# Attention with its queries, keys and values laid out by the host, in a fused attention and mixture-of-experts kernel

## The chip, the cores and the metric

One core of one Trainium2 chip runs the whole program. The metric is device time in microseconds (us). The engines: PE is TensorE (matmuls; PEld its weight loads), DVE is VectorE, ACT is ScalarE, POOL is GpSimd, SP is SyncE, which here only issues transfers. PSUM is the memory that PE writes, SBUF the working memory.

## What is computed

Attention of 2 batches, 8 heads, 576 positions and head size 64 under a mask of blocks of 64, then a gated feed-forward layer, then a mixture of eight experts. Only the inputs of the attention change their form.

```python
def _attn_ref(q, k, v):                      # each (2, 8, 576, 64), float32
    scores = scale * np.matmul(q, k.transpose(0, 1, 3, 2))     # scale = 1/8
    scores = np.where(block_i >= block_j, scores, -1000000000.0)
    scores = scores - np.max(scores, axis=-1, keepdims=True)
    attn = np.exp(scores)
    attn = attn / (np.sum(attn, axis=-1, keepdims=True) + 1e-09)
    return np.matmul(attn, v)
...
x = attn_out as (1152, 512)
x = (x @ w_a) * (x @ w_b) @ w_out            # weights float64, d_ff 1536
return _moe2_ref(x, w_gate, w1, w2, capacity)  # 8 experts, the best one of each token
```

## The kernel before, in words

The program has four stages: attention, the two products with `w_a` and `w_b` (line 418, `prod`), the product with `w_out` (L571), and the experts. PE is the engine that all of them lean on.

**Attention.** Two heads share the 128 partitions, so there are eight *pairs* n = 0 to 7. The host's arrays have positions outside and the 64 head elements inside, whereas a score product needs the head elements on the partitions. So `load_pair` (L166) brings q, k and v in with three transfers each (pieces of 64 elements, 256 bytes); `turn` (L184) turns q or k on PE by five transposes into a PSUM tile `pt`; `q_put` (L191) copies q from there to SBUF on ACT and scales it, `k_put` (L195) copies k on DVE. Then, per pair, four *units* u of score rows, one tile of PSUM each: unit 0 is row tiles 0 and 2, unit 1 is tile 1, unit 2 is tile 3, unit 3 is the last half tile. `score` (L199) makes them on PE, `smax` (L233) takes the row maxima on DVE, `sexp` (L246) the exponentials and sums on ACT into `PB`, `recip` (L263) the reciprocals on DVE, `norm` (L269) multiplies on POOL. Seven groups g of transposes of `PB` (`xpose`, L302) go to PSUM tiles `pT` and are copied to `PTa`/`PTb` by `x_put` (L319): groups 2, 4, 6 on ACT, the rest on DVE. `pv` (L331) multiplies with the values in seven runs; `o_hi` (L348, ACT) and `o_lo` (L352, DVE) write the result split in two parts, `xTh` and `xTl`.

**Rooms.** The pool `psD` has two buffers of two PSUM banks; every score unit, every turned q or k, and the two early products below take one of them in turn. `PB` has two buffers, turned q and k two each, raw q and k three.

**The order is written out by hand** in the table `ORDER`: each word is one step, a letter and its numbers (`steps` in the listing: L load_pair, q/k turn, Q q_put, K k_put, s score, m smax, e sexp, r recip, n norm, t xpose, h x_put, p pv, O o_hi, P o_lo). `s12` is pair 1, unit 2; `p06` is the last run of pair 0's values; `p76` the last of the attention. Each engine does its own part of the words in this order, and waits by itself for what it needs.

**Weights.** `w_a` and `w_b` are float64 read as pairs of int32. Column block f takes `a` (load_wab, two transfers into a `raw` tile of two buffers), `b` (ACT), four DVE steps `c` (`bits64`: L365, L367, L371, L375), `H` (ACT, L402) and `I` (POOL, L408). Blocks 0, 1 and 2 are done among the attention's words. `E0` and `E1` (`ahead`) are the first thirds of the products of blocks 0 and 1, 24 matmuls each, in a `psD` buffer.

**The stage after it** goes over blocks f and thirds c. Per third, PE makes 24 matmuls into two PSUM tiles of three buffers each; `gate_mul` copies one on ACT (`asb`, L486) and multiplies with the other on DVE (`g_sb`, L487), which frees them. The same engines prepare the next blocks of weights there, and `w_out` too (`wor`, `wob`, `woh`: a load, one ACT step, four DVE steps, an ACT cast at L380). The loads of block 3 and of the first `w_out` part stand on SP's queue behind the transfer of `wg_sb`, whose room is that of the attention's tiles.

Of the kernel before, what the change touches and what calls it, by code (L numbers as in the profile page):

```python
# [30 lines left out]


ORDER = """
L00 L01 L10 L11 q0 k0 Q0 L20 K0 q1 s01 Q1 L21 m01 s03 e01 L02 m03 s00 e03 s02 L30 r03 m00 n04 m02 e00 L31 t06
L12 e02 k1 r00 n00 K1 h06 n01 k2 r02 L40 s11 K2 n02 t00 m11 s13 L41 h00 e11 n03 t01 m13 s10 L22 h01 e13 t02 m10
t03 h02 L32 s12 h03 e10 r13 t04 m12 n14 a0 t05 p00 h04 h05 p01 p02 e12 r10 p03 n10 p04 O00 n11 r12 p05 P00 p06
q2 n12 O01 L42 t10 P01 Q2 t11 h10 k3 n13 L50 s21 h11 K3 t16 m21 s23 h16 L51 e21 t12 m23 t13 b0 s20 a1 h13 h12
c00 t14 e23 t15 m20 h14 p10 s22 h15 e20 r23 p11 m22 p12 n24 p13 O10 r20 p14 e22 c01 n20 p15 p16 P10 q3 n21 L52
c02 O11 t26 Q3 n22 k4 P11 h26 s31 r22 L60 b1 K4 t20 n23 t21 m31 s33 h20 L61 e31 h21 p20 c03 s30 m33 H0 a2 t22
m30 t23 e33 I0 p21 h23 h22 s32 r33 O20 c10 e30 t24 n34 t25 P20 p22 m32 h24 p23 q4 h25 e32 t36 r30 L70 c11 p24  # L40
n30 h36 r32 p25 n31 c12 p26 Q4 k5 L71 O21 q5 n32 b2 K5 t30 P21 t31 s41 Q5 L62 h30 n33 s43 h31 m41 c13 p30 e41
t32 m43 t33 H1 s40 c20 h32 I1 p31 h33 e43 t34 m40 O30 t35 h34 s42 P30 e40 h35 p32 r43 p33 m42 n44 p34 s51 r40
e42 c21 n40 p35 p36 m51 t46 n41 L72 O31 c22 s53 e51 n42 P31 h46 t40 m53 s50 h40 e53 r42 t41 m50 s52 n43 p40 h41
e50 r53 p41 m52 n54 t42 t43 c23 h42 k6 e52 t44 h43 p42 r50 t45 h44 K6 n50 q6 O40 h45 t56 n51 H2 p43 P40 r52 n52
h56 p44 Q6 p45 p46 t50 O41 n53 s61 P41 s63 h50 m61 I2 t51 m63 e61 t52 p50 h51 h52 s60 e63 t53 r63 m60 t54 n64
s62 h54 h53 e60 t55 m62 t66 p51 p52 h55 h66 p53 r60 e62 p54 n60 p55 n61 p56 O50 k7 r62 O51 P50 q7 n62 P51 t60 K7
Q7 t61 h60 n63 s71 h61 s73 m71 e71 p60 m73 t62 e73 t63 s70 h62 h63 r73 s72 n74 m70 t64 m72 e70 t65 p61 p62 h65
p63 e72 t76 r70 n70 E0 h64 n71 r72 O60 h76 n72 P60 n73 t70 t71 h70 p64 h71 p65 p66 t72 O61 t73 P61 h72 p70 h73
t74 t75 h74 p71 h75 p72 O70 p73 P70 p74 p75 p76 E1 O71 P71
"""  # L50


# [13 lines left out]
@with_exitstack  # L66
def fused_kernel(ctx: ExitStack, tc, q, k, v, w_a, w_b, w_out, w_gate, w1, w2, consts, out, cap):
    nc = tc.nc
    B, H, S, D = q.shape
# [4 lines left out]
    BLK = 64
    NB = S // BLK
    NP = H // 2
    NPAIR = B * NP
# [69 lines left out]
    PB, V2, QK = [], [], []
    for s in range(3):
        t = att1.tile([P, 2, NTT, 2, D], F32, name=f"QK{s}")
        nc.vector.memset(t[BLK:, :, NQ], 0.0)  # L150
        QK.append(t)
# [12 lines left out]
    qkv, qT, kT, two, one, soft, pxs, ptx = {}, {}, {}, {}, {}, {}, {}, {}

    def load_pair(n, j):  # L166
        b, p = divmod(n, NP)
        if j == 0:
            qkv[n] = QK[n % 3]
        src = (q, k, v)[j]  # L170
        t = V2[n % 4] if j == 2 else qkv[n][:, j]
        full = S // P
# [6 lines left out]
        eng.dma_start(
            out=t[0:S % P, full, :, :],  # L180
            in_=src[b, 2 * p:2 * p + 2, full * P:S, :].rearrange("h p d -> p h d"),
        )

    def turn(n, j):  # L184
        t = qkv[n]
        pt = psD.tile([P, 1024], F32, tag="two", name=f"pt{n}_{j}")
        for tt in range(NTT):
            nc.tensor.transpose(pt[:, tt * P:tt * P + P], t[:, j, tt].rearrange("p h d -> p (h d)"), ident)
        two[n, j] = pt[:, 0:S]
# [862 lines left out]
```

## Time and profile before

| | |
|---|---|
| median of 3 runs | 511.78 us (510.99 to 513.92) |
| the profiled execution: its time / its span | 514.79 us / 513.0 us |
| granted PE clock over the span | 0.958 of full speed |
| busy: PE / DVE / ACT / POOL | 466.8 / 257.8 / 189.6 / 127.4 us |
| turning transposes L188: matmuls, busy | 80, 14.1 us |
| `k_put` L197 on DVE / `q_put` L193 on ACT | 6.0 us / 5.3 us |

The span is what the trace covers, the time is what the run took, 1.8 us more. PE's matmuls overlap in the trace, so the busy time of a group is more than the room it takes on PE; that room is read from one start to the next in a list in order of time.

### The profile page before, as it was taken

Reading aid. Unit: us, or ns where it says so; the run is one execution under the profiler, and the core shown is the slowest. Engines: PE = TensorE matmul, PEld = TensorE weight load, DVE = VectorE, ACT = ScalarE, POOL = GpSimd, SP = SyncE. Lnnn points to the kernel's source line nnn. Section 1 sums busy time; section 2 is a strip of 40 time slices with the busy share of each in tenths; the row PEclk is TensorE's granted clock in tenths of the full one; section 3 lists DMA queues with packets and bytes.
Section 4 is the critical chain, followed back from the end, with each engine's and each line's share of the span. In section 5 each row is a group of like instructions: output and inputs, shape, how many; then the busy total and the mean of one; then the engine's idle time right before and its main releaser. Section 6 shows DMA issues by size and latency. Waiting matters only on the chain. (4 is left out here: it accounts for less than half of the span.)

```text
span 513.0 us, 7684 instructions
## 1 busy us (share of the span) xinstructions
PE 466.8 (91%) x2808; PEld 376.8 (73%) x2808; DVE 257.8 (50%) x513; ACT 189.6 (37%) x391; POOL 127.4 (25%) x134
## 2 busy tenths in 40 slices
PE   5799899999998999999999999996297988999994
PEld 3466556678998999999997777773296787796541
DVE  2679997743647475655332544544365091260111
ACT  2477777643333333332231232221253271341211
POOL 1445777430313131313010110011110120102111
PEclk9799999999998999999999999999577998999998
DMA  8656510005446464654009910000796280451990
GB/s 166 156 154 164 151 26 2 1 1 167 164 145 225 145 225 145 227 205 144 1 2 371 383 44 22 21 26 2 226 289 252 60 315 20 146 221 57 348 324 5
DMA packets 67481, 73.70 MB, mean 144 GB/s; under 512 B 31410, under 2 KB 43826, under 8 KB 67424
## 3 DMA queue, kind: packets, MB, share of 16 engines
q1 hardware_dynamic: 64624, 69.26, 42.2%
q0 software_dynamic: 1456, 3.29, 1.7%
q8 instruction: 29, 0.48, 0.4%
q10 hardware_dynamic: 1344, 0.44, 0.4%
q14 instruction: 28, 0.23, 0.2%
HBM read 62.58 MB, written 11.72 MB: 145 GB/s over the span
## 5 line engine op out<-in xcount | busy, mean ns | idle before, releaser
L418 PE MATMUL p<-xTh,hi 128*128 128x384 f32 x272 | 91.8, 338 | 3.3 <-ACT asb L486 2.1
L418 PE MATMUL p<-xTl,hi 128*128 128x384 f32 x272 | 91.7, 337 | 0.0
L418 PE MATMUL p<-xTh,lo 128*128 128x384 f32 x272 | 91.6, 337 | 0.0
L278 POOL TENSOR_TENSOR PB<-PB,rs 128x576 f32<-128x576 f32 (+4 forms) x40 | 52.4, 1334 | 43.7 <-DVE rs L267 35.7
L418 PEld LDWEIGHTS p<-xTh,hi 128*128 128x128 f32 x272 | 51.6, 190 | 4.2 <-ACT asb L486 2.8
L418 PEld LDWEIGHTS p<-xTh,lo 128*128 128x128 f32 x272 | 51.6, 190 | 0.0
L418 PEld LDWEIGHTS p<-xTl,hi 128*128 128x128 f32 x272 | 51.5, 189 | 0.0
L571 PE MATMUL py<-woh,gh 128*128 128x512 f32 x108 | 45.4, 421 | 0.0
L865 PE MATMUL pH<-xt,whi 128*128 128x288 f32 x192 | 42.1, 313 | 2.8 <-ACTq L910 1.2
L571 PE MATMUL py<-woh,gl 128*128 128x512 f32 x108 | 42.5, 394 | 0.0
L571 PE MATMUL py<-wol,gh 128*128 128x512 f32 x108 | 42.3, 391 | 0.0
L897 PE MATMUL pO<-whi,ht 128*128 128x512 f32 (+1 forms) x112 | 40.1, 428 | 0.0
L253 ACT ACTIVATE PB<-sc,nm 128x256 f32<-128x256 f32 (+3 forms) x64 | 33.1, 531 | 17.7 <-DVE nm L242 12.2
L211 PE MATMUL sc<-k,q 64*64 64x288 f32 (+4 forms) x192 | 36.4, 487 | 2.6 <-ACT PB L258 1.3
L865 PEld LDWEIGHTS pH<-xt,whi 128*128 128x128 f32 x192 | 33.1, 201 | 4.4 <-ACTq L910 1.6
L381 POOL TENSOR_TENSOR wol<-wob,woh 128x1024 fp32r<-128x1024 f32 x6 | 14.4, 2406 | 86.5 <-ACT woh L380 86.5
L242 DVE TENSOR_REDUCE nm<-sc 128x2 f32<-128x512 f32 (+4 forms) x40 | 31.2, 802 | 8.7 <-PE sc L218 4.8
L408 POOL TENSOR_TENSOR lo<-bits,hi 128x1024 fp32r<-128x1024 f32 x12 | 28.7, 2389 | 24.7 <-ACT hi L402 24.7
L487 DVE TENSOR_TENSOR g_sb<-asb,p 128x384 f32<-128x384 f32 x34 | 18.3, 551 | 30.4 <-PE p L418 16.4
L839 POOL DMA_INDIRECT out<-y,ti x12 | 11.4, 946 | 87.9 <-ACT y L904 62.7
L776 DVE TENSOR_TENSOR wlo<-wraw,whi 128x1024 fp32r<-128x1024 f32 x24 | 29.1, 1222 | 6.6 <-ACT whi L775 6.5
L309 PE MATMUL pT<-cst,PB 128*128 128x128 f32 x200 | 29.9, 285 | 0.6 <-POOL PB L278 0.6
(130 smaller groups left out, 789.2 us busy)
## 6 DMA issues: line engine op xcount, KB each, us to landing
wraw<-in_moe_w SPq DMA_DIRECT2D x32, 1024.0 KB, 11.4
raw<-in_moe_w_a SPq DMA_DIRECT2D x12, 512.0 KB, 3.9
raw<-in_moe_w_b SPq DMA_DIRECT2D x12, 512.0 KB, 5.9
wor<-in_moe_w_out SPq DMA_DIRECT2D x6, 1024.0 KB, 6.8
xdisp<-zrow SPq DMA_DIRECT2D x6, 774.0 KB, 7.7
out<-zrow SPq DMA_DIRECT2D x3, 768.0 KB, 7.6
QK<-in_q SPq DMA_DIRECT2D x16, 128.0 KB, 2.6
V<-in_v SPq DMA_DIRECT2D x16, 128.0 KB, 2.8
```

What stands on the lines that cost most here:

```text
L211: nc.tensor.matmul(dst, lhsT=qT[n][hs, P * i:min(P * i + P, S)], rhs=kT[n][hs, c0:c0 + cw], start=True, stop=(i == LAST), skip_group_check ...
L242: nc.vector.tensor_reduce(out=soft[n][0][:, c:c + cnt], in_=view, op=ALU.max, axis=AX.X if i < NQ else AX.XY, negate=True)
L253: nc.scalar.activation(out=dst[:, h], in_=view[:, h], func=AF.Exp, bias=nm[:, c + h:c + h + 1], accum_out=sm[:, c + h:c + h + 1],)
L278: nc.gpsimd.tensor_tensor(out=x, in0=x, in1=r, op=ALU.mult)
L309: nc.tensor.transpose(pt[:, j * P:(j + 1) * P], tile_at(n, i, kt, h), ident)
L408: nc.gpsimd.tensor_tensor(out=lo, in0=f32(m), in1=f32(hi), op=ALU.subtract)
L418: nc.tensor.matmul(ps, lhsT=lt, rhs=rt, start=(n_ == 0), stop=(n_ == len(seq) - 1))
L487: nc.vector.tensor_tensor(out=g_sb[:, f, c * CH:(c + 1) * CH], in0=asb, in1=pb, op=ALU.mult)
L571: nc.tensor.matmul(s["py"], lhsT=lt[:, f], rhs=rt[:, f], start=(f == 0 and i == 0), stop=(f == NF - 1 and i == 2))
L776: nc.vector.tensor_tensor(out=lo[:, a:a + 2], in0=raw[:, a:a + 2], in1=f32(hi[:, a:a + 2]), op=ALU.subtract)
L865: nc.tensor.matmul(ph[:, 0:n].rearrange("p (g c) -> p g c", c=G), lhsT=lt, rhs=rt, start=(n_ == 0), stop=(n_ == len(seq) - 1),)
L897: nc.tensor.matmul(po[:2 * m if tail else m], lhsT=lt, rhs=rt, start=(f == 0 and i == 0), stop=(f == KF2 - 1 and i == len(seq) - 1),)
```

## The change

The host lays out q and k as (pair, 128 partitions of head elements, 576 positions), and v as (pair, position in tile, tile, head, element) with zeros behind the last half tile. Each is then loaded by one transfer, in one piece of 2304 or 2560 bytes per partition. `turn`, `q_put` and `k_put` are gone with their PSUM tiles. The scale of q is a step `Q` in place: on ACT for pair 0, on POOL (`tensor_scalar`, 128x576) for the others. q and k have four buffers each. The clearing of tile ends (DVE for q and k, POOL for v) falls away. `ORDER` is a new table: a pair's units now mostly come as 2, 0, 1, 3, and `E1` stands ahead of the last pair's later transposes.

```diff
 ORDER = """
-L00 L01 L10 L11 q0 k0 Q0 L20 K0 q1 s01 Q1 L21 m01 s03 e01 L02 m03 s00 e03 s02 L30 r03 m00 n04 m02 e00 L31 t06
...
+L00 L01 L10 L11 L20 Q0 L21 s02 Q1 L02 s00 m02 L30 Q2 m00 e02 L31 a0 e00 s01 r02 n03 m01 e01 s03 Q3 r00 s12 L12
...
     def load_pair(n, j):
-        b, p = divmod(n, NP)
...
-        eng = nc.scalar if (n, j) == (0, 1) else nc.sync
-        for h in range(2):
-            eng.dma_start(
-                out=t[:, 0:full, h, :],
-                in_=src[b, 2 * p + h, 0:full * P, :].rearrange("(t p) d -> p t d", p=P),
-            )
...
-    def turn(n, j):
...
-    def q_put(n):
-        qT[n] = att.tile([P, S], F32, tag="q", name=f"q{n}")
-        nc.scalar.activation(out=qT[n], in_=two.pop((n, 0)), func=AF.Copy, scale=scale)
-
-    def k_put(n):
-        kT[n] = att.tile([P, S], F32, tag="k", name=f"k{n}")
-        nc.vector.tensor_copy(out=kT[n], in_=two.pop((n, 1)))
+
+        if j == 2:
+            nc.sync.dma_start(out=V2[n % 4], in_=v[n])
+            return
+        t = att.tile([P, S], F32, tag="qk"[j], name=f"{'qk'[j]}{n}", bufs=4)
+        (nc.scalar if (n, j) == (0, 1) else nc.sync).dma_start(out=t, in_=(q, k)[j][n])
+        (qT, kT)[j][n] = t
+
+    def q_scale(n):
+        if n == 0:
+            nc.scalar.mul(out=qT[n], in_=qT[n], mul=scale)
+        else:
+            nc.gpsimd.tensor_scalar(out=qT[n], in0=qT[n], scalar1=scale, scalar2=None, op0=ALU.mult)
...
+def lay_out(name, a):
...
+    a = a.reshape(b * h // 2, 2, s, d)
+    if name != "v":
+        return a.transpose(0, 1, 3, 2).reshape(-1, P, s)
```

Three places of the order, by engine. In the names, `pt` is a turned q or k, `sc_U` a score unit U, `pT_G` a transpose group, `px` a values product, `early` an early product, `p` a product of the next stage.

PE from its first instruction, before:

```order
L188 MATMUL pt_0_124<-cst,QK_94 128x128 x5
L188 MATMUL pt_1_130<-cst,QK_94 128x128 x5
L188 MATMUL pt_0_143<-cst,QK_96 128x128 x5
L211 MATMUL sc_1_149<-k_141,q_136 128x256 x2
L218 LDWEIGHTS hide
L218 MATMUL sc_1_149<-hide 128x64
```

and now, to the first unit of pair 1 (`q_106`):

```order
L188 MATMUL sc_2_115<-k_104,q_102 128x512 x2
...
L188 MATMUL sc_0_122<-k_104,q_102 128x128 x2
...
L188 MATMUL sc_1_151<-k_104,q_102 128x256 x2
...
L188 MATMUL sc_3_162<-k_104,q_102 64x288 x4
L188 MATMUL sc_2_170<-k_108,q_106 128x512 x2
```

The three turns ahead of the first score are gone, and a score of pair 1 follows pair 0's four units at once.

DVE beside the bit steps of weight block 0, before:

```order
L371 SCALAR_TENSOR_TENSOR bits_433<-raw_323,bits_433 128x1024
L354 TENSOR_TENSOR xTl<-px_1_482,xTh 128x320
L266 TENSOR_SCALAR rs_409<-sm_408 128x2
L267 RECIPROCAL rs_409<-rs_409 128x2
L197 COPY k_544<-pt_1_524 128x576
L242 TENSOR_REDUCE nm_555<-sc_1_532 128x2
L324 COPY PTa_514<-pT_0_546 128x512
L324 COPY PTa_514<-pT_1_552 128x2x128
L375 SCALAR_TENSOR_TENSOR bits_433<-raw_323,bits_433 128x1024
```

and now:

```order
L348 SCALAR_TENSOR_TENSOR bits_258<-raw_144,bits_258 128x1024
L301 COPY PTa_299<-pT_1_346 128x2x128
L219 TENSOR_REDUCE nm_306<-sc_1_359 128x2
L331 TENSOR_TENSOR xTl<-px_1_324,xTh 128x320
L219 TENSOR_REDUCE nm_306<-sc_3_365 128x1
L301 COPY PTb_300<-pT_3_373 128x2x256
L243 TENSOR_SCALAR rs_308<-sm_307 128x6
L244 RECIPROCAL rs_308<-rs_308 128x6
L352 SCALAR_TENSOR_TENSOR bits_258<-raw_144,bits_258 128x1024
```

The copy of k is gone; the bit steps stand among pair 2's steps (`nm_306`) instead of pair 3's (`nm_555`).

PE at the end of the attention, before (`early_1286` is E1, `PB_102` pair 7):

```order
L309 MATMUL pT_5_1264<-cst,PB_102 128x128 x3
L337 MATMUL px_0_1255<-PTa_1182,V_110 64x128 x2
L337 MATMUL px_1_1273<-PTb_1183,V_110 64x320 x6
L337 MATMUL px_1_1273<-PTb_1183,V_110 64x192 x2
L337 MATMUL px_1_1273<-PTb_1183,V_110 64x64 x2
L418 MATMUL early_1286<-xTh,hi_746 128x384
```

and now (`early_1080` is E1, this its last matmul):

```order
L395 MATMUL early_1080<-xTh,lo_633 128x384
L286 MATMUL pT_3_1107<-cst,PB_96 128x128 x4
L286 MATMUL pT_4_1112<-cst,PB_96 128x128 x4
L314 MATMUL px_0_1118<-PTa_1043,V_101 64x256 x2
L286 MATMUL pT_5_1122<-cst,PB_96 128x128 x3
L286 MATMUL pT_6_1126<-cst,PB_96 128x128 x4
L314 MATMUL px_0_1118<-PTa_1043,V_101 64x128 x2
L314 MATMUL px_1_1137<-PTb_1044,V_101 64x320 x6
L314 MATMUL px_1_1137<-PTb_1044,V_101 64x192 x2
L314 MATMUL px_1_1137<-PTb_1044,V_101 64x64 x2
L395 MATMUL p_0_1_1197<-xTh,hi_421 128x384
```

E1 moved from behind the last values product to ahead of the last pair's transpose groups 3 to 6; the next stage's first product now follows the values product.

## Rows read from the trace of the kernel before

**Rows 1.** Page, 40 equal slices of 12.8 us: granted PE clock in tenths, GB/s moved.

```profile
PEclk9799999999998999999999999999577998999998
GB/s 166 156 154 164 151 26 2 1 1 167 164 145 225 145 225 145 227 205 144 1 2 371 383 44 22 21 26 2 226 289 252 60 315 20 146 221 57 348 324 5
```

**Rows 2.** PE in order of time, first 33 us: start, length, instructions, [idle before].

```profile
4.81 1.09 PE L188 MATMUL pt<-cst,QK 128*128 128x128 f32 x4 [4.81 <-DMA QK<-in_q]
...
9.81 1.23 PE L211 MATMUL sc<-k,q 64*128 64x256 f32 x4
...
18.02 0.77 PE L188 MATMUL pt<-cst,QK 128*128 128x128 f32 x5 [1.23 <-ACT PB L253]
...
30.57 2.22 PE L337 MATMUL px<-PTb,V 128*64 128x320 f32 x20
```

**Rows 3.** The same view, one round of a pair, and the end of pair 4.

```profile
32.72 0.77 PE L188 MATMUL pt<-cst,QK 128*128 128x128 f32 x5
...
38.00 0.49 PE L211 MATMUL sc<-k,q 64*128 64x128 f32 x4
...
39.21 0.98 PE L309 MATMUL pT<-cst,PB 128*128 128x128 f32 x7
...
40.71 1.13 PE L211 MATMUL sc<-k,q 64*128 64x512 f32 x4
...
41.80 0.44 PE L337 MATMUL px<-PTa,V 128*64 128x128 f32 x4
...
44.22 0.76 PE L188 MATMUL pt<-cst,QK 128*128 128x128 f32 x5
44.82 0.60 PE L309 MATMUL pT<-cst,PB 128*128 128x128 f32 x4
...
81.89 1.74 PE L337 MATMUL px<-PTb,V 128*64 128x320 f32 x16
```

**Rows 4.** Busy us by stretch: PE, PEld, DVE, ACT, POOL (x count), PEclk, DMA, GB/s.

```profile
40.00:50.00 10.00, 9.99 (x84) 6.09 (x84) 9.39 (x19) 7.65 (x22) 7.27 (x5) 1.00 0.63 179
50.00:60.00 10.00, 9.13 (x75) 6.01 (x72) 9.72 (x18) 8.41 (x22) 6.57 (x5) 1.00 0.57 160
60.00:70.00 10.00, 9.29 (x73) 5.01 (x71) 9.96 (x19) 6.93 (x21) 6.93 (x4) 1.00 0.23 51
70.00:80.00 10.00, 9.56 (x77) 5.89 (x79) 9.90 (x18) 7.32 (x24) 7.30 (x6) 1.00 0.14 31
```

**Rows 5.** Groups by line and shape, 28 to 118 us: busy us, mean ns | idle before.

```profile
L278 POOL TENSOR_TENSOR PB<-PB,rs 128x576 f32<-128x576 f32 x7 | 8.5, 1210 | 15.7 <-DVE rs L267 10.3 <-ACT PB L253 5.4
...
L371 DVE SCALAR_TENSOR_TENSOR bits<-raw,bits 128x1024 int32<-128x1024 int32 x3 | 5.3, 1756 | 0.0
...
L375 DVE SCALAR_TENSOR_TENSOR bits<-raw,bits 128x1024 int32<-128x1024 int32 x3 | 5.2, 1738 | 0.0
...
L197 DVE COPY k<-pt 128x576 f32<-128x576 f32 x5 | 3.7, 738 | 0.0
...
L365 DVE TENSOR_SCALAR bits<-bits 128x1024 f32<-128x1024 f32 x3 | 2.8, 928 | 0.0
...
L367 DVE TENSOR_SCALAR bits<-bits 128x1024 int32<-128x1024 int32 x3 | 2.0, 652 | 0.0
```

**Rows 6.** PE in order of time where the attention ends.

```profile
115.75 0.44 PE L418 MATMUL early<-xTh,hi 128*128 128x384 f32 x1
...
121.36 0.44 PE L418 MATMUL p<-xTh,hi 128*128 128x384 f32 x1 [1.16 <-DVE g_sb L487]
```

**Rows 7.** In order of time, start of the next stage: ACT, DVE, DVE, PE.

```profile
123.90 1.13 ACT L363 ACTIVATE bits<-raw 128x1024 f32<-128x1024 f32 x1 [3.19 <-DMA raw<-in_moe_w_b]
...
126.52 1.23 DVE L371 SCALAR_TENSOR_TENSOR bits<-raw,bits 128x1024 int32<-128x1024 int32 x1
...
143.01 1.01 DVE L487 TENSOR_TENSOR g_sb<-asb,p 128x384 f32<-128x384 f32 x2
...
160.92 0.44 PE L418 MATMUL p<-xTh,hi 128*128 128x384 f32 x1 [1.84 <-ACT asb L486]
```

More of the change, by code (lines that the diff above doesn't have):

```diff
@@ L33 @@
 ORDER = """
-L00 L01 L10 L11 q0 k0 Q0 L20 K0 q1 s01 Q1 L21 m01 s03 e01 L02 m03 s00 e03 s02 L30 r03 m00 n04 m02 e00 L31 t06
[L35 to L48, printed above, removed]
@@ L49 @@
-t74 t75 h74 p71 h75 p72 O70 p73 P70 p74 p75 p76 E1 O71 P71
+L00 L01 L10 L11 L20 Q0 L21 s02 Q1 L02 s00 m02 L30 Q2 m00 e02 L31 a0 e00 s01 r02 n03 m01 e01 s03 Q3 r00 s12 L12
+m03 n00 e03 n01 L40 m12 s10 L41 n02 r03 e12 t00 L22 m10 t01 n04 s11 a1 h00 e10 Q4 m11 t02 h01 p00 r12 t03 h02
+n13 s13 e11 h03 L32 b0 t04 r10 m13 L50 n10 t05 s22 h04 c00 n11 L51 e13 t06 h05 n12 p01 r13 h06 t10 m22 O00 s20
+n14 b1 h10 p02 P00 Q5 e22 m20 p03 p04 c01 p05 e20 p06 t11 r22 L42 t12 c02 n23 s21 O01 s23 h11 h12 m21 t13 P01
@@ new lines @@
+e21 L60 m23 t14 p10 h13 L61 h14 p11 r20 s32 e23 c03 n20 O10 t15 n21 r23 t16 H0 a2 m32 s30 n22 h16 h15 e32 t20
+P10 n24 t21 m30 p12 p13 I0 h20 e30 p14 h21 p15 r32 p16 t22 c10 L52 t23 O11 n33 h22 s31 P11 h23 s33 m31 Q6 t24
+c11 e31 L70 t25 m33 p20 h24 L71 h25 p21 e33 s42 r30 c12 O20 n30 t26 b2 n31 s40 r33 m42 h26 n32 t30 P20 e42 t31
+m40 p22 n34 p23 h30 p24 e40 Q7 p25 h31 r42 p26 t32 c13 L62 n43 t33 O21 s41 h32 h33 s43 H1 m41 P21 t34 e41 I1 m43
+t35 p30 h34 c20 p31 e43 t36 h35 s52 O30 r40 h36 r43 n40 P30 s50 m52 n41 p32 n42 m50 e52 p33 p34 c21 p35 e50 n44
@@ new lines @@
+p36 r52 t40 c22 L72 t41 n53 s51 O31 h40 s53 m51 t42 h41 e51 m53 t43 p40 P31 h42 h43 p41 e53 t44 r50 t45 O40 c23
+n50 s62 h44 n51 h45 H2 t46 r53 n52 s60 m62 h46 p42 P40 n54 e62 m60 p43 p44 I2 r62 p45 e60 p46 t50 t51 h50 s61
+O41 h51 n63 s63 m61 P41 e61 t52 m63 t53 h52 r60 s72 h53 e63 n60 t54 n61 r63 t55 m72 h54 p50 n62 p51 h55 t56 e72
+s70 n64 O50 r72 s71 h56 P50 n73 t60 m70 t61 p52 m71 e70 p53 h60 p54 h61 p55 p56 t62 e71 t63 O51 s73 r70 h62 h63
+n70 P51 t64 n71 m73 t65 h64 E0 n72 h65 e73 r73 n74 t66 t70 h66 p60 h70 p61 p62 O60 p63 P60 p64 p65 p66 t71 O61
@@ L50 @@
+t72 h71 E1 P61 h72 t73 t74 h73 p70 h74 t75 t76 h75 p71 h76 O70 p72 P70 p73 p74 p75 p76 O71 P71
 """
@@ L68, in fused_kernel @@
     nc = tc.nc
-    B, H, S, D = q.shape
+    NPAIR, _, S = q.shape
+    D = P // 2
     NTOK, DM = out.shape
+    B = NTOK // S
     DFF = w_a.shape[1] // 2
@@ L75, in fused_kernel @@
     NB = S // BLK
-    NP = H // 2
-    NPAIR = B * NP
+    NP = NPAIR // B
     KD = DM // P
@@ L145, in fused_kernel @@
         nc.vector.memset(hide[BLK * h:BLK * h + 1, P:P + BLK], -float(1 << 30))
[L147 to L151, printed above, removed]
+    PB, V2 = [], []
     for s in range(2):
@@ L157, in fused_kernel @@
         t = att1.tile([P, NQ + 1, 2, BLK], F32, name=f"V2{s}")
-        nc.gpsimd.memset(t[BLK:, NQ], 0.0)
         V2.append(t)
@@ L162, in fused_kernel @@
     PT = {}
-    qkv, qT, kT, two, one, soft, pxs, ptx = {}, {}, {}, {}, {}, {}, {}, {}
+    qT, kT, one, soft, pxs, ptx = {}, {}, {}, {}, {}, {}
     def load_pair(n, j):
-        b, p = divmod(n, NP)
[L168 to L172, printed above, removed]
-        eng = nc.scalar if (n, j) == (0, 1) else nc.sync
-        for h in range(2):
-            eng.dma_start(
-                out=t[:, 0:full, h, :],
-                in_=src[b, 2 * p + h, 0:full * P, :].rearrange("(t p) d -> p t d", p=P),
-            )
[L179 to L182, printed above, removed]
-    def turn(n, j):
[L185 to L189, printed above, removed]
-    def q_put(n):
-        qT[n] = att.tile([P, S], F32, tag="q", name=f"q{n}")
-        nc.scalar.activation(out=qT[n], in_=two.pop((n, 0)), func=AF.Copy, scale=scale)
-    def k_put(n):
-        kT[n] = att.tile([P, S], F32, tag="k", name=f"k{n}")
-        nc.vector.tensor_copy(out=kT[n], in_=two.pop((n, 1)))
+        if j == 2:
[9 more added lines that the diff above has]
+            nc.gpsimd.tensor_scalar(out=qT[n], in0=qT[n], scalar1=scale, scalar2=None, op0=ALU.mult)
     def score(n, u):
@@ L429, in fused_kernel @@
     steps = dict(
-        L=load_pair, q=lambda n: turn(n, 0), k=lambda n: turn(n, 1), Q=q_put, K=k_put,
+        L=load_pair, Q=q_scale,
         s=score, m=smax, e=sexp, r=recip, n=norm, t=xpose, h=x_put, p=pv, O=o_hi, P=o_lo,
@@ L1020 @@
 _INS = ["q", "k", "v", "moe_w_a", "moe_w_b", "moe_w_out", "moe2_w_gate", "moe2_w1", "moe2_w2"]
+def lay_out(name, a):
+    import numpy as np
+    if name not in ("q", "k", "v"):
+        return a
+    b, h, s, d = a.shape
+    assert 2 * d == P
+    a = a.reshape(b * h // 2, 2, s, d)
+    if name != "v":
+        return a.transpose(0, 1, 3, 2).reshape(-1, P, s)
+    a = np.pad(a, ((0, 0), (0, 0), (0, -s % P), (0, 0)))
+    return a.reshape(a.shape[0], 2, -1, P, d).transpose(0, 3, 2, 1, 4)
 def kernel(**inputs):
@@ L1035 @@
     for name in _INS:
-        a = np.ascontiguousarray(inputs[name])
+        a = np.ascontiguousarray(lay_out(name, inputs[name]))
         wide = a.dtype == np.float64
```

## The prediction

> **What bounds the kernel now.** I first asked where the change can act: only in the attention and at its seam with the next stage. The page's slices show a granted clock near 2.4 GHz in the attention but for a dip to 0.7 of it in the second slice [rows 1]. Then I read PE in order of time over the attention, because all later stages wait for its last product. It falls into four pieces.
>
> *Start.* PE waits until 4.81 for q, turns three tiles, and makes its first score at 9.81; the last values run of pair 0 (p06) ends at 30.57 + 2.22 = 32.8 [rows 2]. In between PE stands still again and again, and its clock goes down to 1.2 GHz for a while, which is the dip of rows 1. The first slice moves only 166 GB/s, though the page has slices of 371 and 383 [rows 1]: the pieces of 256 bytes load slowly.
>
> *A round.* From 32.72 to 44.22, one whole pair, no row shows a wait: 11.50 us [rows 3]. Five transposes of a turn take 44.82 − 44.22 = 0.60, so the two turns of a pair cost PE 1.2 us and a round without them is 10.3.
>
> *The middle.* From 40 to 80 us PE is busy 9.1 to 10.0 of 10, but DVE 9.39 to 9.96: 38.97 of 40 us [rows 4]. There the weight blocks' bit steps stand beside the softmax. DVE is the bound here and PE waits for it, a little at a time. The last run of pair 4 (p46) ends at 81.89 + 1.74 = 83.6 [rows 3].
>
> *The end.* From 83.6 to T = 115.75, where E1 starts right behind p76 [rows 6], PE is the bound.
>
> **The change, part by part.** I work out T', the new end of p76, piece by piece.
>
> *Loads and first score.* q0, k0, and the constants are some 720 KB. At the 371 to 383 GB/s of the best slices [rows 1] they take 2 us. The old first pieces of q held PE until 4.81 [rows 2]; the new loads are larger but in pieces of 2304 bytes. Bounds: 3.5 us (half the wait goes) to 6 us (k0 shares the rings with the pairs behind it). I take 4.5, and 0.5 for scaling q0 on ACT: first score at **5.0** instead of 9.81.
>
> *From the first score to p06.* Before 32.8 − 9.8 = 23.0. Out go the turns of k1 and k2, 0.77 each as they ran [rows 2]: −1.5. In come two units of pair 2, which now stand before p06: 39.21 − 38.00 = 1.2 and 41.80 − 40.71 = 1.1 [rows 3]: +2.3. The scaling on POOL: no row shows it. Its nearest row is POOL's product of the same 128x576, 1.21 us with two inputs [rows 5]; I take 1.2, bounds 0.5 and 2.5. Three of the seven, Q1 to Q3, find POOL waiting for the first reciprocals. Q4 stands in POOL's queue ahead of n13 and the normalization of pair 1, and waits for a load that itself waits until pair 0's scores have left their buffer: +1.2. Sum 25.0, so p06 ends at **30.0**. The scores are handed from PE to DVE to ACT through two PSUM buffers as before, so the pace is not set by the turns alone; that is why I keep the old interval and only exchange its parts.
>
> The Trainium skill's GPSIMD Engine Reference (4.1 Engine selection) calls an elementwise operation with one input roughly line-rate there: by it a scaling would take some 0.5 us, an estimate from 576 elements at the 1.2 GHz of its section 1, and p06 would come 0.7 earlier. No trace here shows it.
>
> *From p06 to p46.* If DVE is the bound, its work counts. In the 40 us of rows 4 it was busy 39.0; that held two copies of k (0.74 each [rows 5]) and eleven of the twelve bit steps. A block's four steps last 0.93 + 0.65 + 1.76 + 1.74 = 5.1 [rows 5]; eleven of them, c01 to c23, 14.3, or 13.3 since each overlaps its follower by about 0.1. The rest, 39.0 − 1.5 − 13.3 = 24.2, is what the pairs need. PE's pace was (83.6 − 44.2) / 3 = 13.1 us a pair there, so 40 us hold 3.05 pairs: 7.9 us of DVE a pair. In the new order the stretch from p06 to p46 holds four pairs and, again, eleven bit steps (one stands before p06): 4 × 7.9 + 13.3 = 44.9, at the share of 39.0 / 40 that it reached 46.1. PE needs only about 41 for the same words: four rounds of 10.3. So the transposes and copies come out, and DVE stays the bound. Before, this stretch took 83.6 − 32.8 = 50.8. New p46: 30.0 + 46.1 = **76.1**, 7.5 earlier.
>
> *From p46 to p76.* PE is the bound, 115.75 − 83.6 = 32.2. Out: two turns, −1.2, and two units of pair 6, which now stand before p46, −2.3. In: one transpose group, +0.5, and E1, 121.36 − 1.16 − 115.75 = 4.45 [rows 6]. Sum 33.6, **T' = 109.7**, 6.05 before T. The old q copies on ACT (one a pair) cost nothing here or earlier: DVE and PE hide them. E1 fills the waits of the last pair's transposes, so I add nothing for those.
>
> *The seam.* Before, E1 covered the copies behind p76, and PE went on at 121.36 = T + 5.6. Now these copies lie bare: xTh, asb, asb, g_sb follow p76, and the first product waits for the second g_sb because it takes E1's banks. Before, the row of chain was the same but for E1; I count 2.4 us, so PE goes on at T' + 2.4. E1's move thus looks like another 3.2 us won. **I cost it at nothing**, because of what comes next: the loads of weight block 3 and w_out stand on SP's queue behind p76 in both orders. From them a chain of loads, ACT and DVE steps runs without PE: bits at 123.90, two g_sb at 143.01, and a copy that PE waited for 1.84 us until 160.92, which is T + 45.2 [rows 7]. PE can be ahead by three thirds of a block only. If it comes 3.2 earlier, it waits 3.2 longer, in part already for the g_sb at T + 27.3, and goes on at T' + 45.2 all the same. From there to the end everything moves with T'.
>
> So the sum is −6.05 us. The profiled execution lies 3.0 above the median, its span 1.2 above. From 511.8: **505.7 us** (in an execution like the profiled one a span of 507).
>
> **The rivals.** I call under 0.5% (2.6 us, 509.2 and 514.3) the same, about what a measurement of this kernel tells apart.
>
> *E1's move counts.* If the chain of weights behind p76 is quicker than I read it, or PE was not held by it alone, the 3.2 us of the seam are kept: 502.5. For it: of this chain only the 1.84 us were seen as a wait of PE. Against: the steps before them wait for loads, not for PE [rows 7].
>
> *DVE gives way.* If the new order spreads DVE's steps so that PE bounds the middle, the stretch takes 42 instead of 46.1: 501.6. Against: bit steps still end with pair 4, and the later pairs have none.
>
> *POOL slows DVE.* The bit step of L371 lasts 1.76 us in the attention and 1.23 at 126.52, where POOL stands idle [rows 5, 7]. Seven scalings, 8.4 us more of POOL, could lengthen DVE steps beside them by up to the same 43%: 3.6 us, all on the bound of the middle, 509.3. Against: most of DVE's steps there read PSUM or one small tile. The Trainium skill's GPSIMD Engine Reference (1. Specifications) says that GpSimd shares its SBUF interface with VectorE, which contends when a VectorE instruction reads two SBUF inputs; with the pair 1.76 and 1.23 the trace agrees.
>
> *The clock, the other side.* With the turns gone PE has less to do between pair 0's units, and a clock that fell after a wait of 1.23 us at 18.02 [rows 2] could stay at 1.2 GHz from the first score to p06. PE has there a round without turns, 10.3, four units of pair 1 (some 4.1) and 2.3 for pair 2, 16.7 at full speed, 33.4 at half: p06 at 38.4 instead of 30.0, and 514.1. A fall or two more in the middle, where PE waits for DVE, or a stretch over 9 us longer, and it is slower: 515. Against: before, the worst slice still got 0.7 of full speed [rows 1], and DVE and ACT set much of the pace there anyway.
>
> That the transposes are not really gone is excluded: the order shows no L188 of before.
>
> **How the numbers follow.** My forecast 0.55, with 503 to 508.5 from the bounds of load, scaling and DVE's share; E1's move 0.16; DVE gives way 0.10; POOL slows DVE 0.08; the clock 0.06, most of it slower; 0.05 for a mixture that I don't see, of either sign. Two in ten outside: the range reaches from below the two quicker cases, 500.5, to 509.8 above the POOL case. Faster by over 0.5%: the forecast, both quicker cases and part of the rest, 0.84. Same: 0.11. Slower: 0.05.
>
> **What would show it.** Right: the first score near 5 us, p06 near 30, p46 near 76, p76 near 110; DVE busy over 9 of 10 from 35 to 75; in the next stage PE waits longer than 1.84 in all before it goes on about 45 us behind p76. Wrong: DVE with gaps in the middle while PE is full; PE running through the seam with no longer waits; a clock of 0.5 over most of the first 30 us; scalings on POOL over 2.5 us.

## The result and the profile after

Median 505.24 us of 4 runs (502.47 to 505.81), before 511.51 of 4 on the same chip: ratio 0.9854, interval 0.9816 to 0.9891. Predicted were 505.7 and faster. I ran the changed kernel three times more as a control beside the experiments: 503.04, 504.31 and 502.65, with ratios 0.9780 [0.9741, 0.9818], 0.9821 [0.9787, 0.9855] and 0.9776 [0.9743, 0.9809]; the medians lie 10.3, 9.1 and 12.2 us below those of the kernel before on the same chip. So the gain is rather 9 to 12 us than the 6.3 of the first comparison, and my 6.05 was too small. That the first median met my number to half a microsecond is chance; the steps are judged one by one below. One run of e3_old_order (524.56) and one of e4_scale_act (2470.47) lie far above the others of their kernel and are left out of the ratios; without them the medians in the table below would be 516.97 and 503.22.

The page of after, clock and transfers by slices of 12.5 us, to lay beside [rows 1]:

```profile
PEclk9799999999999999999999999998598999999998
...
GB/s 312 208 123 158 28 26 2 1 34 220 128 171 199 169 194 179 190 239 114 2 92 389 318 22 21 22 25 3 245 320 218 149 237 22 222 155 82 361 307 3
```

The first slice now moves 312 GB/s, before 166. The dip of the clock in the second slice is still there (what the clock does ahead of it the page doesn't show; see the last rival below).

PE of after in order of time (start, length, then what it waited for), the marks of [rows 2, 3, 6, 7]:

```profile
5.62 2.08 PE L188 MATMUL sc<-k,q 64*128 64x512 f32 x4 [5.62 <-DMA k<-in_k]
...
12.88 4.19 PE L188 MATMUL sc<-k,q 64*64 64x288 f32 x12 [1.58 <-ACT PB L230]
...
28.92 2.27 PE L314 MATMUL px<-PTb,V 128*64 128x320 f32 x20
...
73.23 2.27 PE L314 MATMUL px<-PTb,V 128*64 128x320 f32 x20
...
106.25 2.27 PE L314 MATMUL px<-PTb,V 128*64 128x320 f32 x20 [0.31 <-ACT PTb L299]
110.81 0.41 PE L395 MATMUL p<-xTh,hi 128*128 128x384 f32 x1 [2.28 <-DVE g_sb L464]
...
151.74 0.44 PE L395 MATMUL p<-xTh,hi 128*128 128x384 f32 x1 [1.65 <-ACT asb L463]
```

First score 5.62; p06 ends at 28.92 + 2.27 = 31.19, p46 at 75.50, p76 at 108.52. PE goes on at 110.81 and, after the second wait, at 151.74. Before, the latter was 160.92 [rows 7], so 9.2 us are won by there. The spans of the two profiled executions lie 12.5 us apart (513.0 and 500.5). The other 3.3 fall behind that mark, where both kernels do the same steps; the four profiles of the changed kernel differ by 2.8 there among themselves.

The middle of after by stretches, to be read as [rows 4]:

```profile
30.00:40.00 10.00, 10.00 (x85) 6.41 (x83) 9.90 (x21) 8.37 (x26) 8.29 (x6) 1.00 0.47 151
40.00:50.00 10.00, 9.62 (x80) 5.65 (x76) 9.90 (x19) 6.80 (x20) 9.18 (x6) 1.00 0.44 140
50.00:60.00 10.00, 9.36 (x80) 6.04 (x80) 9.93 (x17) 8.38 (x24) 8.91 (x6) 1.00 0.13 34
60.00:70.00 10.00, 8.30 (x71) 5.09 (x68) 9.86 (x21) 5.95 (x21) 7.32 (x5) 1.00 0.12 34
70.00:80.00 10.00, 10.00 (x78) 5.85 (x78) 8.88 (x19) 8.26 (x24) 9.51 (x7) 1.00 0.01 2
```

DVE (the third of the five busy times) stands at 9.9 of 10 from 30 to 70, and PE (the first) has gaps there. That reads as if DVE bound the middle more firmly than before; e5 and e9 below test it.

Groups of after by line and shape, 8 to 100 us (as [rows 5]):

```profile
L174 POOL TENSOR_SCALAR q<-q 128x576 f32<-128x576 f32 x6 | 10.7, 1787 | 0.3 <-DMA q<-in_q 0.3
...
L255 POOL TENSOR_TENSOR PB<-PB,rs 128x576 f32<-128x576 f32 x8 | 9.6, 1201 | 1.0 <-DVE rs L244 1.0
...
L352 DVE SCALAR_TENSOR_TENSOR bits<-raw,bits 128x1024 int32<-128x1024 int32 x3 | 3.9, 1312 | 0.0
...
L342 DVE TENSOR_SCALAR bits<-bits 128x1024 f32<-128x1024 f32 x3 | 3.8, 1256 | 0.0
L348 DVE SCALAR_TENSOR_TENSOR bits<-raw,bits 128x1024 int32<-128x1024 int32 x3 | 3.6, 1215 | 0.0
...
L344 DVE TENSOR_SCALAR bits<-bits 128x1024 int32<-128x1024 int32 x3 | 2.4, 804 | 0.0
```

The scaling takes 1.79 us on POOL, longer than the product of the same shape with two inputs. The four bit steps of a block sum to 1.26 + 0.80 + 1.22 + 1.31 = 4.6 us, before 5.1.

### The profile page after: what moved, and what is told of

It reads as the page before. It is cut to its first block, busy times and chain, and to the rows that moved or that the text cites. A ratio compares the mean times of both kernels' runs of the same rounds, so it can differ in the third digit from the quotient of the medians.

```text
span 500.5 us, 7435 instructions
## 1 busy us (share of the span) xinstructions
PE 452.5 (90%) x2728; PEld 365.6 (73%) x2728; DVE 250.1 (50%) x502; ACT 185.9 (37%) x384; POOL 139.6 (28%) x137
## 5 line engine op out<-in xcount | busy, mean ns | idle before, releaser
L255 POOL TENSOR_TENSOR PB<-PB,rs 128x1024 f32<-128x1024 f32 (+4 forms) x40 | 53.5, 1362 | 14.8 <-DVE rs L244 12.5
L188 PE MATMUL sc<-k,q 64*64 64x288 f32 (+4 forms) x192 | 37.9, 508 | 9.5 <-DMA k<-in_k 5.6
L548 PE MATMUL py<-wol,gh 128*128 128x512 f32 x108 | 42.3, 391 | 0.0
L230 ACT ACTIVATE PB<-sc,nm 128x512 f32<-128x512 f32 (+3 forms) x64 | 33.0, 528 | 20.6 <-DVE nm L219 17.3
L874 PE MATMUL pO<-whi,ht 128*128 128x512 f32 (+1 forms) x112 | 39.0, 418 | 0.0
L219 DVE TENSOR_REDUCE nm<-sc 128x2 f32<-128x1024 f32 (+4 forms) x40 | 31.2, 801 | 10.3 <-PE sc L195 9.2
L626 POOL DMA_INDIRECT xdisp<-row,sl x9 | 9.0, 1004 | 81.6 <-ACT row L555 77.0
```

The source lines that it names most:

```text
L188: nc.tensor.matmul(dst, lhsT=qT[n][hs, P * i:min(P * i + P, S)], rhs=kT[n][hs, c0:c0 + cw], start=True, stop=(i == LAST), skip_group_check ...
L219: nc.vector.tensor_reduce(out=soft[n][0][:, c:c + cnt], in_=view, op=ALU.max, axis=AX.X if i < NQ else AX.XY, negate=True)
L230: nc.scalar.activation(out=dst[:, h], in_=view[:, h], func=AF.Exp, bias=nm[:, c + h:c + h + 1], accum_out=sm[:, c + h:c + h + 1],)
L255: nc.gpsimd.tensor_tensor(out=x, in0=x, in1=r, op=ALU.mult)
L548: nc.tensor.matmul(s["py"], lhsT=lt[:, f], rhs=rt[:, f], start=(f == 0 and i == 0), stop=(f == NF - 1 and i == 2))
L874: nc.tensor.matmul(po[:2 * m if tail else m], lhsT=lt, rhs=rt, start=(f == 0 and i == 0), stop=(f == KF2 - 1 and i == len(seq) - 1),)
```

## The experiments

All are edits of the changed kernel. In the diffs of `ORDER` only the words around a moved one stand. *Own control* is the changed kernel run again beside it on the same chip. p46 and p76 are ends by the profile of one execution. "Go on" is PE's first product behind the seam; where E1 stands behind p76, PE makes E1 before it. The *second go-on* is PE's first product behind its later wait, for the copy `asb`.

| kernel | median us | ratio to before | own control | p46 | p76 | go on |
|---|---|---|---|---|---|---|
| e0_control | 503.04 | 0.9780 | | 75.15 | 108.17 | 110.46 |
| e1_E1_behind | 500.36 | 0.9726 [0.9687, 0.9765] | 503.04 | 76.43 | 105.78 | 111.30 |
| e2_loads_early | 499.70 | 0.9707 [0.9669, 0.9745] | 503.04 | 74.88 | 107.91 | 110.20 |
| e3_old_order | 517.16 | 1.0055 [1.0026, 1.0083] | 503.04 | 88.91 | 125.58 | 131.13 |
| e0b_control | 504.31 | 0.9821 | | 75.71 | 108.74 | 111.03 |
| e4_scale_act | 503.54 | 0.9795 [0.9756, 0.9835] | 504.31 | 75.45 | 108.46 | 110.75 |
| e5_block2_late | 506.27 | 0.9860 [0.9824, 0.9896] | 504.31 | 73.13 | 111.02 | 113.31 |
| e7_old_order_act | 503.55 | 0.9819 [0.9782, 0.9855] | 504.31 | 75.94 | 107.21 | 112.75 |
| e0c_control | 502.65 | 0.9776 | | 75.31 | 108.33 | 110.62 |
| e8_behind_early | 499.67 | 0.9718 [0.9687, 0.9750] | 502.65 | 75.55 | 104.90 | 110.43 |
| e9_block2_spread | 496.56 | 0.9656 [0.9624, 0.9689] | 502.65 | 73.53 | 102.88 | 108.41 |
| e10_old_order_early | 503.40 | 0.9773 [0.9739, 0.9807] | 502.65 | 77.71 | 108.98 | 114.52 |

**The control.**

> The changed kernel once more, as the yardstick for the runs beside it on the same chip. Both theories: 505 us, within 1.5, ratio 0.987 to the kernel before.

> The changed kernel again, as the yardstick on this chip: ratio 0.978 to 0.987 to the kernel before.

> The changed kernel once more, beside which the other three of this call are read. Both theories: 0.978 to 0.988 of the time of the kernel before, p46 near 75.5, p76 near 108.6, and a wait of PE for asb of 1 to 2 us some 43 us behind p76.

Two of the three are a little faster than I expected (for the first I had 503.5 to 506.5). The marks of the four profiles of the changed kernel lie within 0.6 us of each other up to go on, and the second go-on at 151.0 to 151.9.

**E1 moved back behind p76 (e1).**

```diff
-t72 h71 E1 P61 h72 t73 ... p75 p76 O71 P71
+t72 h71 P61 h72 t73 ... p75 p76 E1 O71 P71
```

> Only E1 moves back behind the last values product p76; all else is the new order. Theory A (the chain of weight loads and steps behind p76 sets when PE goes on, some 43 us after p76, and E1 is no longer filler where it is needed): p76 ends about 3.4 us earlier (4.45 less for E1, 1 more for waits of the last pair's transposes that E1 covered), and everything behind follows: 501.8 us, 3.4 below the control. Theory B (E1's early place is worth the 3.2 us that it seemed to save at the seam, and PE's own work sets the stage behind it): 505 to 508 us, not below the control.

2.7 us below its control, and theory B is excluded. PE goes on no earlier at the seam (111.30, though this profiled run made its first score only at 7.42, 1.6 late), but the later wait for `asb` is gone. So E1's place costs time, and not at the seam.

**The loads behind p76 made early (e2).** Block 3's load gets a word behind the last bit step of block 1, and the first part of `w_out` one behind block 2's last.

```diff
-... c13 L62 ... c23 n50 ...
+... c13 a3 L62 ... c23 W0 n50 ...
...
+        E=ahead, W=load_wout,
...
-    load_wab(3)
-    load_wout(0)
```

> The new order, but the loads of weight block 3 and of the first part of w_out are issued inside the attention, as soon as their buffers are free, instead of behind p76. Theory A: the chain behind p76 starts 5.5 us earlier, the wait of 1.65 us of PE some 43 us behind p76 is gone, and PE goes on as its own work allows: 503.5 us, 1.7 below the control. Theory B (the chain does not decide): as the control within 0.5 us.

3.3 us below its control; p76 and the seam are those of the control within 0.3, and again no wait is left behind the seam. The gain is twice what I expected. E1 stays early here, and its cost is gone all the same. So what E1's place costs is that the loads, which stand on SP's queue behind the attention, start later.

**Both at once (e8).**

```diff
-... c13 L62 ... c23 n50 ... h71 E1 P61 ... p76 O71 P71
+... c13 a3 L62 ... c23 W0 n50 ... h71 P61 ... p76 E1 O71 P71
```

> E1 behind p76 again and the loads of block 3 and of the first w_out part early, both at once. Theory A (E1 ahead of p76 costs because it holds up p76, and with it the loads and the chain of weights behind them; each of the two edits takes PE's wait at that chain away): they do not add up. With E1 behind there was no wait for asb left, so the early loads find nothing to shorten: 2.5 to 4 us below the control, as each alone had it (2.7 and 3.3). Theory B (each edit has an effect of its own, E1's covering the copies at the seam and the loads using idle rings): they add, 6 us below the control.

3.0 below its control: the two don't add up, as theory A had it. They remove the same loss, and ACT shows it. Its queue in the control e0c_control at the seam:

```profile
108.70 0.87 ACT L463 COPY asb<-early 128x384 f32<-128x384 f32 x2
114.91 1.12 ACT L340 ACTIVATE bits<-raw 128x1024 f32<-128x1024 f32 x1 [5.34 <-DMA raw<-in_moe_w_b]
115.94 0.47 ACT L463 COPY asb<-p 128x384 f32<-128x384 f32 x1
```

and in e8_behind_early:

```profile
109.69 1.13 ACT L340 ACTIVATE bits<-raw 128x1024 f32<-128x1024 f32 x1
112.85 0.48 ACT L463 COPY asb<-p 128x384 f32<-128x384 f32 x1 [2.03 <-PE p L395]
```

In the control the first step of block 3 holds ACT for 5.34 us while the weights land, and the copy that frees PE's bank stands behind it in the same queue: 115.94. With the weights there, the copy waits for PE instead and runs at 112.85. PE lives on its spare banks for a while and pays later. PE's waits in the control from 104 to 160 us (in total, times, longest):

```profile
PE p L395 <- DVE g_sb L464: 3.2, 2, 2.3
PE p L395 <- ACT asb L463: 1.5, 1, 1.5
```

and in e8:

```profile
PE p L395 <- DVE g_sb L464: 1.2, 1, 1.2
```

This is 3.5 us of waiting less, 3.0 in the time.

**The new layout with the old order (e3).** The old table without the words of turns and copies; scalings on POOL where `q_put` stood.

```diff
-L00 L01 L10 L11 L20 Q0 L21 s02 Q1 L02 s00 m02 ...
+L00 L01 L10 L11 Q0 L20 s01 Q1 L21 m01 s03 e01 ...
```

> The host's layout and the scaling on GpSimd with the old table of steps, from which only the turns and their copies are taken out; E1 is behind p76 as in the kernel before. Theory A (layout and loads bring the time, the new order of units little, and E1's move costs): start 4.2 earlier, two turns 1.5 and two more 1.2 out of PE's path, four copies of k 2.6 out of DVE's, a scaling 1.65 in: p76 about 7.9 earlier than in the kernel before, 503.6 us. Theory C (the new order is needed to get anything for it): 508 to 511 us.

Slower than the kernel before by half a per cent, 14 us above its control, and outside what either theory gave. The profile is of an execution of 521.97, 4.8 above the median, so its marks can lie late by as much. Its PE waited, over the attention:

```profile
PE sc L188 <- POOL q L174: 11.1, 5, 3.2
...
PE pT L286 <- POOL PB L255: 3.4, 5, 1.4
```

and with the waits went the clock (the figure behind the five busy times):

```profile
30.00:40.00 10.00, 8.98 (x49) 5.38 (x49) 4.05 (x7) 4.49 (x11) 2.83 (x2) 0.66 0.49 169
40.00:50.00 10.00, 6.76 (x50) 4.10 (x48) 6.40 (x15) 6.09 (x19) 8.24 (x6) 0.88 0.29 93
...
60.00:70.00 10.00, 6.25 (x34) 3.45 (x35) 7.70 (x9) 4.34 (x9) 10.00 (x6) 0.73 0.12 34
```

The old order asks for a scaled q a few words before its score, and POOL, which works off its normalizations in order, doesn't have it. The layout in the old order, with the scaling on POOL, thus gains nothing.

**The same with the scaling on ACT (e7).**

```diff
-        if n == 0:
-            nc.scalar.mul(out=qT[n], in_=qT[n], mul=scale)
-        else:
-            nc.gpsimd.tensor_scalar(out=qT[n], in0=qT[n], scalar1=scale, scalar2=None, op0=ALU.mult)
+        nc.scalar.mul(out=qT[n], in_=qT[n], mul=scale)
```

> The host's layout with the old table and the scaling on ACT where it was, so that PE no longer waits for GpSimd's scalings (11.1 us in five waits when these stood at the old places). If the layout alone brings the time: start 4.2, turns 2.7 and copies of k 2.6 out, p76 9 earlier than in the kernel before, 503 to 506 us. If the old table can't use it: 508 to 511.

503.55, level with the change (its control 504.31). ACT scales in 0.69 us, at the old place of `q_put`. So with the scaling left on ACT, the layout reaches the whole gain of the change without the new order. How much of it comes from the larger pieces of the loads, and how much from the turns and copies that are gone, wasn't tried. Nor does this yet say what the new order is worth, since E1 stands behind p76 here and ahead of it in the control.

**The old order with the loads early (e10).** As the one before, with the words `a3` and `W0` of the second experiment.

> The new layout with the old order (less turns and copies), scaling on ACT, and the loads early. Theory A: that order already has E1 behind p76 and no wait for asb is left, so the early loads bring less than 1 us: within 1 us of the 0.982 of the same order without them, and 2 us or more above the kernel with the new order, E1 behind and early loads, since its p76 came 1.4 us later than the new order's with E1 behind. Theory B (the new order is worth nothing in itself): level with that kernel.

0.75 above its control, where e7 was 0.76 below its own: by the controls the early loads bring nothing here, where E1 stands behind p76 anyway. Its ratio of 0.9773 is 0.005 below e7's, more than I allowed, but so is that of its control. It lies 3.7 above e8, whose p76 was 104.90, here 108.98. So the new order is worth some 3.7 us once E1 and the loads are out of its way. The two also differ in where the scaling is done; by e4, next, this moves little.

**All scalings on ACT in the new order (e4).** The diff of e7 with the table of the change.

> The new order with every scaling of q on ACT (0.68 us each) instead of GpSimd (1.65 each), at the same places of the table. If the scalings on GpSimd slow DVE beside them or hold up the normalizations: 2 to 3 us below the control. If DVE's own work bounds the middle and GpSimd has room for them: within 1 us of the control.

503.54 against 504.31. Taking seven scalings off POOL and giving ACT some 7 × 0.69 = 4.8 us more moves the time by less than the runs differ: in the new order neither of the two is the bound.

**Block 2's bit steps out of the middle (e5, e9).** Two versions. First, into pairs 5 and 6:

```diff
-... h34 c20 p31 ... p34 c21 p35 ... t40 c22 L72 ... O40 c23 n50 ... p44 I2 r62 ...
+... O50 c20 ... P50 c21 ... p53 c22 ... p56 c23 ... P51 H2 ... n74 I2 ...
```

> The new order with the four bit steps of weight block 2 and its two splits moved from pairs 3 and 4 to pairs 5 and 6, where DVE is idle more than half of the time. If DVE bounds the middle: some 4.6 us of DVE work leave the stretch up to the last run of pair 4, PE needs 41 of its 44.3 us, so that run ends 2.5 to 3 us earlier, and the end 2 to 3 us below the control. If PE or the hand-over of buffers bounds it: within 0.7 us of the control.

Neither expectation held for the time. p46 comes 2.6 us earlier (0.6 of them already at p06), as DVE's bound asks, but p76 comes 2.3 later, and the time is 2.0 above the control. e5's stretches:

```profile
70.00:80.00 10.00, 10.00 (x85) 6.15 (x79) 8.15 (x20) 7.58 (x24) 6.58 (x6) 1.00 0.01 2
80.00:90.00 10.00, 6.76 (x56) 4.46 (x56) 9.66 (x15) 5.72 (x21) 3.59 (x4) 0.94 0.01 2
```

The four steps fell between 79.7 and 89.5, DVE is the bound there, and PE waits for it:

```profile
88.13 1.42 PE L286 MATMUL pT<-cst,PB 128*128 128x128 f32 x8 [3.24 <-DVE PTa L301]
```

The trouble was where they went, not that they went. So the second version, on top of e8, puts them where the trace shows DVE idle, behind the last reciprocals of pair 7:

```diff
-... h34 c20 p31 ... p34 c21 p35 ... t40 c22 L72 ... O40 c23 W0 n50 ... p44 I2 r62 ...
+... r73 c20 c21 c22 n74 ... P60 c23 W0 p64 ... h72 H2 I2 t73 ...
```

> As the kernel with E1 behind and the loads early, and block 2's four bit steps and two splits put where DVE and ACT stand idle by the trace (three steps at 92.4 to 96, the fourth near 100) instead of bunched into pair 5. Theory A (DVE's work bounds the middle, and only its bunching gave the gain back in the kernel that moved these steps into pairs 5 and 6): p46 near 73, p66 and p76 2 to 2.6 us before those of the kernel with the steps in place, and the end as much earlier. Theory B (the gain up to p46 is lost again because pairs 5 to 7 run at their own pace, set by the hand-over of scores between PE, DVE and ACT, or because PE then waits for block 2): p46 near 73 but p76 and the end unchanged within 1 us.

496.56, 3.1 below e8, 6.1 below the control and 3.4% below the kernel before: the best of all. p46, p66 (96.26 for 98.26) and p76 each come 2.0 us earlier. e8 in the middle, and then e9:

```profile
60.00:70.00 10.00, 8.30 (x73) 5.09 (x68) 9.86 (x22) 5.91 (x21) 7.32 (x5) 1.00 0.14 42
70.00:80.00 10.00, 10.00 (x79) 5.90 (x79) 8.89 (x19) 8.26 (x24) 9.46 (x7) 1.00 0.33 107
```

```profile
60.00:70.00 10.00, 10.00 (x85) 6.13 (x79) 8.20 (x18) 6.77 (x22) 7.38 (x7) 1.00 0.13 43
70.00:80.00 10.00, 10.00 (x84) 6.19 (x83) 8.16 (x19) 7.42 (x23) 6.58 (x6) 1.00 0.01 2
```

PE goes from 8.30 to 10.00 and DVE falls to 8.2: with block 2 gone the bound passes to PE, which is why nearly 5 us of DVE's work give only 2. From p06 to p46 it is 73.53 − 31.23 = 42.3 us, in e8 44.3.

## Why the prediction was right, step by step

| mark | predicted | after | its three controls |
|---|---|---|---|
| first score | 5.0 | 5.62 | 5.66 to 5.82 |
| p06 ends | 30.0 | 31.19 | 30.86 to 31.42 |
| p46 ends | 76.1 | 75.50 | 75.15 to 75.71 |
| p76 ends, T' | 109.7 | 108.52 | 108.17 to 108.74 |
| PE goes on | T' + 2.4 | T' + 2.29 | T' + 2.29 |
| second go-on | T' + 45.2 | T' + 43.2 | T' + 42.7 to 43.2 |
| median us | 505.7 | 505.24 | 502.65 to 504.31 |

*Start.* 0.6 late, inside my bounds of 3.5 to 6 for the load: the score waits for k0 (`in_k` in the first row above). Whether the loads behind k0 held it up isn't shown. From there to p06 25.6 us for 25.0. My sum left out that `ORDER` also puts one transpose group of pair 1, t10, ahead of p06, 0.5 us by what I took for a group elsewhere; the clock, below, is the other candidate.

*The scaling on POOL.* Mis-sized: 1.2 taken, 1.65 in the shortest, 1.79 in the mean of six. It stayed inside the bounds, and POOL hid it in the new order (e4). The 0.5 us that I worked out from the Trainium skill's GPSIMD Engine Reference (4.1 Engine selection) was further off: with one input it is slower here than with two.

*The middle.* The reason was right: DVE at 9.9 of 10, p46 2 us earlier with block 2 taken out (e5, e9), hardly with POOL relieved (e4). The term was 46.1 and measured 75.50 − 31.19 = 44.3. From 31.0 to 75.5 DVE was busy 43.6 of 44.5 us, where I had 44.9 at a share of 0.974; the share reached is 0.98. The work is less for two reasons. The bit steps of a block took 4.6 us for 5.1, and ten of them fall into the stretch, not the eleven that I counted: `ORDER` has c00 and c01 ahead of p06, and c01 ended at 30.92.

*End of the attention.* 33.0 for 33.6.

*The seam and E1.* The seam's 2.4 was right, and so was the chain of weights that sets the second go-on at a fixed distance from p76. "I cost it at nothing" stands beside 4.45 us of E1 in the sum ahead of p76, and by the chain those are lost outright. I didn't say that the move is a loss; e1, e2 and e8 show 2.7 to 3.3 us of it. At p76 itself it costs 108.33 − 104.90 = 3.4 (e8), not 4.45: the rest seems to fall into waits of the last pair that are there anyway.

*The wait.* PE was to wait 3.2 us longer than the 1.84 of before, 5.0 in all behind the seam. It waited 1.65 in after and 1.6 to 2.7 in the controls, so the sign that I named for this, more than 1.84, failed in two of four profiles. The chain still decides, but with 1.6 to 2.7 us to spare. It was itself 2.0 to 2.5 shorter (next step): 5.0 less that is 2.5 to 2.8 for e0_control and e0c_control, where 2.7 and 2.4 were measured. In the other two profiles the clock fell behind the seam (last section), so PE's own work took longer and it waited less.

*The distance itself* was the largest miss, 2.0 us. In the kernel before, ACT's first step on block 3 began 123.90 − 115.75 = 8.2 us behind p76 [rows 6, 7], after the change 115.29 − 108.52 = 6.8, in the controls 6.6 to 7.0. The new order of SP's queue is the same there; also in e7, with the old order, it is 114.19 − 107.21 = 7.0. The loads were issued 0.9 us behind p76 in both kernels (116.68 and 109.40); what differs is how long they took to land, the first of them (`w_a`) 5.7 us before and 4.3 after, 3.9 to 4.2 in the controls. This gives 1.4 of the 2.0. Why the transfers took longer in the one profile of the kernel before stays open, and so does the other 0.6.

Together: 1.2 from the earlier T' and 2.0 from the distance make 9.2 won at the second go-on instead of 6.05. The three later comparisons, 9.1 to 12.2 us in the times, agree with that. So the path was right and two of its terms, the middle and the distance, were too long; that the first comparison came out at 6.3 hid both.

*The rivals.* E1's move does not count as a gain: excluded by e1. DVE giving way: not as the change stands, but e9 shows what it would have looked like (42.3 us in the middle, where that rival had 42). POOL slowing DVE over the whole middle: the bit steps got shorter, though POOL was busier, and with the scalings off POOL the stretch from p06 to p46 is only 0.6 shorter than in the control (75.45 − 31.73 = 43.7 in e4). The clock: it was lower at the start than the page says, before and after. In these traces the record of the clock begins 3 to 13 us behind PE's first product, and what lies ahead of it is printed as full speed. In e0c_control it begins at 17.6 us, and the stretch from 10 to 20 reads 1.00; but a score unit of the same shape takes 1.22 us there and 0.70 later:

```profile
10.60 1.22 PE L188 MATMUL sc<-k,q 64*128 64x256 f32 x4 [0.68 <-ACT PB L230]
...
20.38 0.70 PE L188 MATMUL sc<-k,q 64*128 64x256 f32 x4 [0.82 <-ACT PB L230]
```

So by the lengths PE ran at the lower level there, as it did for the first score of before (1.23 for the same shape, [rows 2]). My reading of one dip in the second slice was too kind. Of the four profiles of the changed kernel, e0b_control was slow the longest, to some 19 us, and e0_control the shortest, to 10.2 and from 13.6 to 17.0; from the first score to p06 they took 25.7 and 25.0. So this rival's 8.4 us did not come: 5.5 us more at the lower clock go with 0.7 more up to p06, since PE waits for the hand-over of scores there (the waits for `PB` in these rows).

## What to carry to other kernels

Where an in-order engine both prepares later data and frees the bound engine's buffers, a late load blocks the second through the first, here for 3 us: look what stands behind a waiting step in its queue, and start the load early rather than shift work around it. Work that isn't due can leave the stage that its engine bounds, but only to where the trace shows that engine idle; bunched, it gives back more than it won. Before an engine takes over a small step, ask how many words lie between the step and its reader: the same scaling on POOL was free in one order and cost some 14 us in the other.

## What the runs showed that I had not expected

A DVE step on the weights depends on when it begins beside POOL. In after, DVE:

```profile
30.24 0.68 DVE L344 TENSOR_SCALAR bits<-bits 128x1024 int32<-128x1024 int32 x1
...
57.13 2.33 DVE L342 TENSOR_SCALAR bits<-bits 128x1024 f32<-128x1024 f32 x1
...
65.18 1.22 DVE L348 SCALAR_TENSOR_TENSOR bits<-raw,bits 128x1024 int32<-128x1024 int32 x1
```

and POOL:

```profile
29.39 2.05 POOL L174 TENSOR_SCALAR q<-q 128x576 f32<-128x576 f32 x1
...
54.70 1.89 POOL L255 TENSOR_TENSOR PB<-PB,rs 128x1024 f32<-128x1024 f32 x1
56.55 2.36 POOL L385 TENSOR_TENSOR lo<-bits,hi 128x1024 fp32r<-128x1024 f32 x1
...
65.43 2.72 POOL L255 TENSOR_TENSOR PB<-PB,rs 128x1024 f32<-128x1024 f32 x1 [0.39 <-ACT PB L230]
```

The step of L342 takes 0.69 us where POOL stands idle. Begun at 57.13 inside POOL's instruction of 56.55 to 58.91, it ended at 59.46, 0.55 behind it; in e5 a step of L344 begun at 82.08 beside POOL's product of 82.02 to 83.91 took 2.38 and also ended 0.55 behind. The step of L348 that began 0.25 ahead of POOL's product took its usual 1.22, and the product took 2.72 for 1.89. It looks as if the later one waits for the earlier, where POOL's instruction has two inputs. It doesn't hold beside POOL's scaling, which has one: the step begun at 30.24 inside the scaling of 29.39 to 31.44 took its usual 0.68. Of the twelve bit steps of the attention, seven began inside one of POOL's products before, and four after. That the shorter bit steps of the new order come from this is read from the starts and wasn't tried by itself.

The clock fell to 0.50, 1.2 GHz, from 112 to 114 us in after and in e0b_control, behind a wait of 2.28 and 2.29 us at the seam, but stayed at 1.00 in e0_control and e0c_control, behind waits of 2.29 and 2.28. So the length of the wait alone doesn't tell whether it falls.
